# An mLSTM and MoE kernel: the decays' exponents from a TensorE product in place of a DMA broadcast

## The chip, the cores and the metric

The kernel runs on one core of a Trainium2 chip. The core has five engines with instruction queues of their own: PE (matrix products, results to PSUM), DVE, ACT and POOL (elementwise work and reductions) and SP, which here issues all DMA transfers; 16 DMA engines carry them. The metric is the time of one execution in microseconds of the device. Before the change it is 322.91 us, the median of three runs (322.81 to 323.3).

## The reference

Two stages follow each other. The first is a recurrent cell over 768 steps for 4 batches x 8 heads, head size 40, with gates that decay the state; the second is a feed-forward layer over the 3072 tokens with 320 features, 1024 hidden units, an activation h x softmax(h) and a layer norm.

```python
for t in range(S):
    m_new = np.maximum(f_gate[:, :, t] + m, i_gate[:, :, t])
    f_stab = np.exp(f_gate[:, :, t] + m - m_new)
    i_stab = np.exp(i_gate[:, :, t] - m_new)
    m = m_new
    C = f_stab[..., None, None] * C + i_stab[..., None, None] * np.einsum('bhd,bhe->bhde', vt, kt)
    n = f_stab[..., None] * n + i_stab[..., None] * kt
    h_tilde = np.einsum('bhde,bhe->bhd', C, qt)
    denom = np.maximum(np.abs(np.einsum('bhd,bhd->bh', n, qt)[:, :, None]), 1.0)
    y[:, :, t] = sigmoid(o_gate[:, :, t]) * h_tilde / denom
x = y.transpose(0, 2, 1, 3).reshape(B * S, H * D)
h = x @ w_in
e = np.exp(h - max(h)); solu = h * e / (sum(e) + 1e-09)
out = (solu - mean(solu)) / sqrt(var(solu) + 1e-06) * g_ln @ w_out
```

## The kernel before

The recurrence is worked in chunks of 128 steps, so there are 24 units: 4 batches x 6 chunks, chunk by chunk over the batches. With G the running sum of the forget exponents inside a chunk and I the input gate relative to the running maximum, step t sees step s of its chunk with the weight exp(G[t] + I[s] - G[s]) for t >= s, and 0 else.

**Head of the program.** The gates lie as 32 rows (batch and head) of 768 steps. Two scans on DVE (lines 393 and 409) give the maximum and G. G is stored to DRAM (tile gd, line 419). POOL subtracts to get I - G, PE transposes I - G and G, DVE copies both to bG (line 458), and ACT takes the exponential of the G half (line 461). Beside it the weights arrive as 64-bit words: ACT, DVE and PE decode, split, centre and scale them (load_w_in, load_w_out, centre_w_out, scale_w_out). Idle products on PE (line 1340) keep its clock up until the output weights' means are formed.

**One unit.** SP loads the tokens tk (v, k, q; line 803) and **gb** (line 804): G of the unit's chunk, 8 heads x 128 steps, read from DRAM into all 128 partitions. DVE finds the largest value of a token, am (line 829), ACT and DVE split k and q into two half-precision parts qs, and SP transposes them to qT by DMA (line 873). POOL writes -1e30 into gb where t < s (line 889). ACT makes the weights d: one exponential per head with I - G as the bias of each partition (line 904), and before the mask dec, the decay of the whole chunk, from gb's last column (line 885). PE forms the scores from qT into a PSUM tile sy (946), DVE multiplies them by am and d into p (958), PE multiplies p by the values into sy (1008) and qT by the state cs (982). DVE divides, giving x, and POOL multiplies by the sigmoid of the output gates sg (line 1058). For the next chunk POOL scales k by d's last column (kt, 926), PE multiplies it by the values (1072), POOL decays the state (ct, 1082), DVE adds (1094), POOL splits the state into parts (1107, 1116), and SP copies them across partitions (1122, 1123). Then the layer: PE transposes x (1132), 16 matmuls of 128x512 give ph (1185), DVE takes the negated row maximum nm (1201), ACT and DVE form e and its statistics, POOL takes a power (pw, 1262) and splits e into us (1277), SP transposes us by DMA into big (1282), and 24 matmuls give the output (1305).

**Order.** A planner (class Plan) simulates the engines with a cost for each operation and issues, on each engine, the ready operation of the lowest rank. Ranks come from the table RANK, one row per engine and tile, as base, slope at the head and slope at the tail. Nothing is reordered at run time. PSUM tiles are shared: sy has two buffers, sx and so_ one each, ph two.

Of the kernel before, what the change touches and what calls it, by code (L numbers as in the profile page):

```python
# [8 lines left out]
F32 = mybir.dt.float32  # L9
# [5 lines left out]
ALU = mybir.AluOpType  # L15
# [318 lines left out]
def mlstm_moe_kernel(ctx: ExitStack, tc: tile.TileContext, tok, og, fg, ig, w_in, w_out, gln, out):  # L334
# [81 lines left out]
    for b in range(B):  # L416
        load(
            300,
            lambda P, b=b: nc.sync.dma_start(
                out=P[("gd", 0)][b].rearrange("c h l -> h c l"),  # L420
                in_=gt(P, G_)[b * H : (b + 1) * H, :].rearrange("h (c l) -> h c l", l=L),
            ),
            [("gd", 0, b)],
            [G_],
            prio=g0,
        )

# [10 lines left out]
        POOL,  # L438
        1790,
        lambda P: nc.gpsimd.tensor_tensor(out=gt(P, I_), in0=gt(P, I_), in1=gt(P, G_), op=ALU.subtract),  # L440
        [I_],
        [G_],
        prio=g0,
    )
    for nm in SMALL:
        P.tag(nm, SMALL[nm], lambda nm=nm: pp.tile([L, 512], F32, name=nm, tag=nm, bufs=SMALL[nm]))

    def tr_gates(P):
        pt = P[("so_", "g")].rearrange("p (a c n) -> p a c n", a=2, c=8)
        for c in range(NC):  # L450
            nc.tensor.transpose(pt[:, 0, c, :], gt(P, I_)[:, c * L : (c + 1) * L], P[I][: B * H, : B * H])
            nc.tensor.transpose(pt[:, 1, c, :], gt(P, G_)[:, c * L : (c + 1) * L], P[I][: B * H, : B * H])

    P.op(PE, 700, tr_gates, [("so_", "g")], [I_, G_, I], prio=g0)


    def mk_bG(P):
        V.tensor_copy(out=P[BG], in_=P[("so_", "g")].rearrange("p (a c n) -> p a c n", a=2, c=8)[:, :, 0:NC, :])
# [14 lines left out]
    cst("wg", [L, NK, DM], F32)  # L473
# [3 lines left out]
    WIH, WIL, WOH, WOL, WG, OW = (("wih", 0), ("wil", 0), ("woh", 0), ("wol", 0), ("wg", 0), ("ow", 0))  # L477

# [23 lines left out]
    def decode(raw, n, key, dst, prio):  # L502
# [14 lines left out]
        def di(P):  # L517
# [21 lines left out]
            [key],  # L539
# [32 lines left out]
    def load_w_in(i, prio):  # L572
# [18 lines left out]
        load(1500, ld, [raw], prio=RANK["sp w_in"][0], behind=[("gb", 0)] if i > 2 else [])  # L591
# [156 lines left out]
    tag("gb", [L, H, L], F32, 2)  # L748
# [37 lines left out]
    def unit(u):  # L786
        b, c = units[u]
        pr = float(u)
        tk, gb, am, rr, qT, d_t = (("tk", u), ("gb", u), ("am", u), ("rr", u), ("qT", u), ("d", u))
# [13 lines left out]
        load(1500, lambda P: nc.sync.dma_start(out=P[tk], in_=tok[b, c * L : (c + 1) * L, :]), [tk], prio=rank(SPQ, "tk"), behind=[("gb", u - 2)] if u > 1 else [])  # L803
        load(1500, lambda P: nc.sync.dma_start(out=P[gb], in_=P[("gd", 0)][b, c].partition_broadcast(L)), [gb], [("gd", 0, b)], prio=rank(SPQ, "gb"))
# [78 lines left out]
        dec = ("dec", u)  # L883
        if 0 < c < NC - 1:
            op(ACT, 110, lambda P: nc.scalar.activation(out=P[dec], in_=P[gb][0:D, :, L - 1], func=AF.Exp), [dec], [gb])  # L885
        op(
# [3 lines left out]
                out=P[gb],  # L890
                in_=P[gb],
# [10 lines left out]
        def decay(P, j):
            for h in range(4 * j, 4 * j + 4):
                nc.scalar.activation(  # L904
                    out=P[d_t][:, h, :],
                    in_=P[gb][:, h, :],
                    func=AF.Exp,
                    bias=P[BG][:, 0, c, b * H + h : b * H + h + 1],
                )
# [11 lines left out]
        kt = ("kt", u)  # L921
# [464 lines left out]
```

## Time and profile before

| | |
|---|---|
| median of 3 runs | 322.91 us (322.81 to 323.3) |
| the profiled execution | 324.31 us, of which the span from first to last instruction is 322.5 us |
| granted PE clock, mean | 0.979 |
| busy share of the span | PE 87%, DVE 82%, ACT 74%, POOL 54% |
| DMA engines, share of their time | 89% |
| moved over the span | 66.66 MB |

A share is an average over a program with different stages. What a unit costs is read from stretches of the span, and from what an engine waited for just before it went on. PE's busy time includes the run-out of each matmul, so that its rate is read from the starts of successive ones.

### The profile page before, as it was taken

Reading aid. Unit: us, or ns where it says so; the run is one execution under the profiler, and the core shown is the slowest. Engines: PE = TensorE matmul, PEld = TensorE weight load, DVE = VectorE, ACT = ScalarE, POOL = GpSimd, SP = SyncE. Lnnn points to the kernel's source line nnn. Section 1 sums busy time; section 2 is a strip of 40 time slices with the busy share of each in tenths; the row PEclk is TensorE's granted clock in tenths of the full one; section 3 lists DMA queues with packets and bytes.
Section 4 is the critical chain, followed back from the end, with each engine's and each line's share of the span. In section 5 each row is a group of like instructions: output and inputs, shape, how many; then the busy total and the mean of one; then the engine's idle time right before and its main releaser. Section 6 shows DMA issues by size and latency. Waiting matters only on the chain.

```text
span 322.5 us, 6918 instructions
## 1 busy us (share of the span) xinstructions
PE 279.7 (87%) x2403; PEld 229.8 (71%) x2403; DVE 264.3 (82%) x671; ACT 239.7 (74%) x505; POOL 174.5 (54%) x186
## 2 busy tenths in 40 slices
PE   0189979697989999897999969999889989999984
PEld 0189868475868888686778848878767767888753
DVE  7978998999999888859969866988889889887740
ACT  2466788989788999649979847987869967635641
POOL 6435152638467847763848655666657655434210
PEclk9999988969999999999999997999999999999999
DMA  7599995899889999999989999999998999634391
GB/s 218 202 250 252 331 255 195 196 259 224 165 255 213 238 187 231 216 250 239 217 200 227 258 208 239 185 233 225 239 200 229 212 241 190 133 66 91 82 155 58
DMA packets 118723, 66.66 MB, mean 207 GB/s; under 512 B 102880, under 2 KB 110016, under 8 KB 118688
## 3 DMA queue, kind: packets, MB, share of 16 engines
q1 hardware_dynamic: 118688, 66.21, 89.0%
q8 instruction: 19, 0.31, 0.4%
q14 instruction: 16, 0.13, 0.2%
HBM read 33.85 MB, written 4.03 MB: 117 GB/s over the span
## 4 chain that ended last, share of the span: by engine, by line
PE 42%; DVE 14%; DMA 14%; issue 13%; POOL 9%; SPq 3%; ACT 3%; POOLq 0%; ACTq 0%; DVEq 0%
PE ph L1185 14%; DMA tk<-in_tok_dram 5%; PE sy L1008 4%; DMA gb<-gd 4%; PE sx L1132 2%; DMA big<-us 2%; POOL x L1058 2%; POOL gb L889 2%; PE sy L946 2%; PE sy L982 2%; PE sx L1072 1%; POOL us L1277 1%; DVE qs L857 1%; DMA out_dram<-ot 1%; DVE wg L547 1%
## 5 line engine op out<-in xcount | busy, mean ns | idle before, releaser
L1305 PEld LDWEIGHTS <-big 128*128 128x128 f16 x576 | 63.2, 118 | 18.0 <-DMA big<-us 3.8
L904 ACT ACTIVATE d<-gb,bG 128x128 f32<-128x128 f32 x192 | 59.0, 390 | 3.5 <-POOL gb L889 1.7
L1008 PEld LDWEIGHTS sy<-tk,p 128*128 128x128 f32 x384 | 57.4, 198 | 2.9 <-DVE p L958 0.3
L849 ACT ACTIVATE qs<-tk,rr 128x640 f16<-128x640 f32 x48 | 37.2, 819 | 26.7 <-DVE rr L842 23.2
L1008 PE MATMUL sy<-tk,p 128*128 128x41 f32 x384 | 56.6, 253 | 0.1
L1277 POOL TENSOR_TENSOR us<-e,us 128x1024 f16<-128x1024 f32 x23 | 49.1, 2139 | 11.0 <-ACT us L1287 10.8
L889 POOL TENSOR_SCALAR_AFFINE_SELECT gb<-gb 128x1024 f32<-128x1024 f32 x24 | 27.3, 1137 | 37.8 <-ACT dec L885 21.7
L829 DVE TENSOR_REDUCE am<-tk 128x1 f32<-128x640 f32 x24 | 19.5, 812 | 21.9 <-DMA tk<-in_tok_dram 21.9
L958 DVE SCALAR_TENSOR_TENSOR p<-sy,am,d 128x512 f32<-128x512 f32 x48 | 35.0, 736 | 2.4 <-PE sy L946 2.3
L1262 POOL TENSOR_TENSOR pw<-ab,mhalf 128x1 f32<-128x1 f32 x24 | 13.2, 551 | 42.4 <-DVE ab L1254 41.9
L1201 DVE TENSOR_REDUCE nm<-ph 128x1 f32<-128x1024 f32 x24 | 29.2, 1217 | 7.1 <-PE ph L1185 6.9
L1185 PE MATMUL ph<-wih,xh 128*128 128x512 f32 x96 | 34.1, 437 | 0.0
L1058 POOL TENSOR_TENSOR x<-x,sg 128x320 f32<-128x320 f32 x24 | 21.8, 908 | 20.3 <-DVE rr L842 7.8
L1243 ACT ACTIVATE sq<-e,nmean 128x1024 bf16<-128x1024 f32 x24 | 27.5, 1146 | 5.8 <-DVE e L1234 5.4
L1234 DVE SCALAR_TENSOR_TENSOR e<-ph,s,e 128x1024 f32<-128x1024 f32 x24 | 30.6, 1273 | 0.9 <-ACT e L1208 0.9
L1208 ACT ACTIVATE e<-ph,nm 128x1024 f32<-128x1024 f32 x24 | 26.6, 1109 | 5.0 <-DVE nm L1201 4.7
L1185 PE MATMUL ph<-wil,xh 128*128 128x512 f32 x96 | 30.1, 394 | 0.0
L857 DVE SCALAR_TENSOR_TENSOR qs<-tk,rr,qs 128x320 f16<-128x320 f32 x48 | 29.0, 633 | 0.5 <-ACT qs L849 0.3
L1287 ACT CAST us<-e 128x1024 f16<-128x1024 f32 x24 | 24.9, 1035 | 2.7 <-issue 2.6
L1185 PE MATMUL ph<-wih,xl 128*128 128x512 f32 x96 | 26.5, 398 | 0.2 <-DVE xl L1143 0.2
L926 POOL TENSOR_TENSOR kt<-tk,d 128x320 f32<-128x320 f32 x20 | 16.5, 829 | 11.9 <-ACT d L904 10.7
L1132 PE MATMUL sx<-ident,x 128*128 128x128 f32 (+1 forms) x72 | 12.8, 289 | 10.7 <-POOL x L1058 5.9
(181 smaller groups left out, 691.7 us busy)
## 6 DMA issues: line engine op xcount, KB each, us to landing
gb<-gd SPq DMA_DIRECT2D x24, 512.0 KB
tk<-in_tok_dram SPq DMA_DIRECT2D x24, 484.0 KB
sg<-in_og_dram SPq DMA_DIRECT2D x12, 320.0 KB
out_dram<-ot SPq DMA_DIRECT2D x24, 160.0 KB
big<-in_w_out_dram SPq DMA_DIRECT2D x4, 640.0 KB
cs<-cs SPq DMA_DIRECT2D x20, 102.5 KB
big<-in_w_in_dram SPq DMA_DIRECT2D x4, 512.0 KB
cs<-c SPq DMA_DIRECT2D x20, 51.2 KB
```

Of the source, the lines that this page charges most:

```text
L849: nc.scalar.activation(out=dst, in_=q_src(P, a).unsqueeze(2).to_broadcast([L, H, 2, D]), func=AF.Copy, scale=P[rr],)
L857: V.scalar_tensor_tensor(out=q_parts(P, a, 2 - a, 1), in0=q_src(P, a), scalar=P[rr], in1=q_parts(P, a, 0, 1), op0=ALU.mult, op1=ALU.subtract,)
L889: lambda P: nc.gpsimd.affine_select(out=P[gb], in_=P[gb], pattern=[[0, H], [1, L]], base=0, channel_multiplier=-1, compare_op=ALU.is_ge, f ...
L904: nc.scalar.activation(out=P[d_t][:, h, :], in_=P[gb][:, h, :], func=AF.Exp, bias=P[BG][:, 0, c, b * H + h : b * H + h + 1],)
L958: lambda P, j=j, ps=ps: V.scalar_tensor_tensor(out=P[p_t][:, 4 * j : 4 * j + 4, :], in0=P[ps].rearrange("p (h l) -> p h l", l=L), scalar=P ...
L1008: nc.tensor.matmul(yv(P)[:, h, :], lhsT=P[p_t][:, h, :], rhs=v1(P)[:, h, :], start=True, stop=True)
L1058: lambda P: nc.gpsimd.tensor_tensor(out=P[x], in0=P[x], in1=P[sg][:, u % OG, :], op=ALU.mult),
L1185: nc.tensor.matmul(P[ph][:, j * 512 : (j + 1) * 512], lhsT=a, rhs=w[:, j * 512 : (j + 1) * 512], start=n == 0, stop=n == 7,)
L1201: lambda P: V.tensor_reduce(out=P[nm], in_=P[ph], axis=AX.X, op=ALU.max, negate=True),
L1234: lambda P: V.scalar_tensor_tensor(out=P[e], in0=P[ph], scalar=P[sc], in1=P[e], op0=ALU.mult, op1=ALU.mult, accum_out=P[nmean]),
L1277: (V if last else nc.gpsimd).tensor_tensor(out=P[us[1]][:, 1], in0=P[e], in1=P[us[0]][:, 0], op=ALU.subtract)
L1305: nc.tensor.matmul(P[po][:, 0:DM], lhsT=uTv(P, a)[:, k, :], rhs=P[w][:, k, :], start=n == 0, stop=n == 23)
```

## The change

The exponent G[t] + I[s] - G[s] becomes a matrix product. Each of the two terms is split into a part rounded to the PE's 32-bit format and the rest. A left operand **el** of 128 rows x 128 steps holds two rows of ones, then two rows for each of the 8 heads with the parts of I - G, and zeros below. A right operand **er** of 128 rows x 8 heads x 128 steps holds in its first two rows the parts of G, below them indicators (one in the rows of the head, zero elsewhere), and zeros in the rest. Two matmuls of 128x512 per unit, four heads each, give the exponents in sy. Rows that never change are written once; per unit SP loads only el's 16 rows and er's 2 rows, 8 KB each, from two DRAM tiles bd and gd.

ACT takes the exponential from PSUM, two instructions of four heads each, with no bias. POOL's mask now works on d, after the exponential, and writes zeros. DVE writes p in place into d, so that the tile p is gone and d has three buffers. The last column of d is copied to dl on ACT before the mask, for kt. The decay of the state no longer comes from gb: a product with a selecting matrix (sel) copies exp(G) of each chunk's last step for all units to 40 partitions at once, in the head (tile DEC). In the head, I - G moves from POOL to DVE, and each of I - G and G gets a copy on ACT and a subtraction on DVE for its parts, and two stores. The state's own arithmetic is unchanged. The gates' scratch rows move into wg, which the output weights fill later.

The core of the diff (of RANK two rows; all others have new numbers too):

```diff
-    "sp gb": (-18.49, -14.13, -3.91),
+    "sp el": (-8.75, 8.76, 2.09),
...
+    def parts(whole, hi, dst):
+        P.op(ACT, 750, lambda P: nc.scalar.copy(out=gt(P, hi).bitcast(F32R), in_=gt(P, whole)), [hi], [whole], prio=g0)
+        P.op(DVE, 870, lambda P: V.tensor_tensor(out=gt(P, whole).bitcast(F32R), in0=gt(P, whole), in1=gt(P, hi), op=ALU.subtract), ...)
+        for n, k in enumerate((hi, whole)):
+            load(100, lambda P, n=n, k=k: nc.sync.dma_start(out=P[dst][:, n], in_=gt(P, k)), [(*dst, n)], [k], prio=g0)
...
+    parts(I_, BT, BD)
+    parts(G_, GH, GD)
...
-        load(1500, lambda P: nc.sync.dma_start(out=P[gb], in_=P[("gd", 0)][b, c].partition_broadcast(L)), ...)
+        load(100, lambda P: nc.sync.dma_start(
+                out=P[el].bitcast(F32)[2 : 2 + 2 * H],
+                in_=P[BD].rearrange("p a s -> (p a) s")[b * 2 * H : (b + 1) * 2 * H, c * L : (c + 1) * L]), ...)
+        load(100, lambda P: nc.sync.dma_start(
+                out=P[er].bitcast(F32)[0:2],
+                in_=P[GD][b * H : (b + 1) * H, :, c * L : (c + 1) * L].rearrange("h a l -> a h l")), ...)
...
+        for j in range(2):
+            pd = ("sy", ("d", u, j))
+            def exponents(P, j=j, pd=pd):
+                nc.tensor.matmul(P[pd], lhsT=P[el], rhs=P[er].rearrange("p h l -> p (h l)")[:, j * 512 : (j + 1) * 512], start=True, stop=True)
+            P.op(PE, 232, exponents, [pd], [el, er], rank(PE, "d"))
+            op(ACT, 600, lambda P, j=j, pd=pd: nc.scalar.activation(
+                    out=P[d_t][:, 4 * j : 4 * j + 4, :], in_=P[pd].rearrange("p (h l) -> p h l", l=L), func=AF.Exp), ...)
+        if c < NC - 1:
+            op(ACT, 115, lambda P: nc.scalar.copy(out=P[dl], in_=P[d_t][:, :, L - 1]), [dl], [(*d_t, 0), (*d_t, 1)])
...
-        for j in range(2):
-            op(ACT, 1170, lambda P, j=j: decay(P, j), [(*d_t, j)], [gb, BG])
...
-        p_t = ("p", u)
+        p_t = d_t
...
-    tag("d", [L, H, L], F32, 2)
+    tag("d", [L, H, L], F32, 3)
```

**What moves in the order.** On PE, in the middle of the program: `so__` is a unit's output product, `ph` the hidden product of the next, `sy<-qT` the scores of the one after. Before:

```order
L1305 LDWEIGHTS big
L1305 MATMUL so__2506<-woh,big 128x320
L1185 MATMUL ph<-wih,xh 128x512 x2
L1185 MATMUL ph<-wil,xh 128x512 x2
L1185 MATMUL ph<-wih,xh 128x512 x2
L1185 MATMUL ph<-wil,xh 128x512 x2
L1185 MATMUL ph<-wih,xl 128x512 x4
L1185 MATMUL ph<-wih,x_2539 128x512 x2
L1185 MATMUL ph<-wil,x_2539 128x512 x2
L1072 MATMUL sx<-tk,kt 40x41 x8
```

The same place after:

```order
L1436 LDWEIGHTS big
L1436 MATMUL so__2404<-woh,big 128x320
L1005 MATMUL sy<-er_97,el_106 128x512
L1316 MATMUL ph<-wih,xh 128x512 x2
L1316 MATMUL ph<-wil,xh 128x512 x2
L1316 MATMUL ph<-wih,xl 128x512 x4
L1005 MATMUL sy<-er_97,el_106 128x512
L1076 LDWEIGHTS qT
L1076 MATMUL sy<-qT 128x128
```

The hidden product was in one piece; now the two exponent matmuls of the next unit stand ahead of it and in it, and the scores of that unit cut it too.

On POOL, one unit of the middle (the mask is AFFINE_SELECT; numbers tell the units apart). Before:

```order
L889 AFFINE_SELECT gb_2287<-gb_2287 128x1024
L1262 TENSOR_TENSOR pw_2457<-ab_2454,mhalf_94 128x1
L1277 TENSOR_TENSOR us_2447<-e_2330,us_2447 128x1024
L1058 TENSOR_TENSOR x_2467<-x_2467,sg_1746 128x320
L926 TENSOR_TENSOR kt_2518<-tk_2194,d_2380 128x320
L1107 TENSOR_TENSOR cs0_2513<-cs0_2513 40x328
L1082 TENSOR_TENSOR ct_2543<-cs1_1963,dec_2072 40x328
L1116 TENSOR_TENSOR c3_2583<-cs0_2513 40x328
```

After:

```order
L1393 TENSOR_TENSOR pw_2204<-ab_2197,mhalf_112 128x1
L1031 AFFINE_SELECT d_2169<-d_2169 128x1024
L1056 TENSOR_TENSOR kt_2237<-tk_1842,dl_2202 128x320
L1213 TENSOR_TENSOR ct_2246<-cs0_1694,dec_208 40x328
L1238 TENSOR_TENSOR cs3_2235<-cs3_2235 40x328
L1247 TENSOR_TENSOR c3_2286<-cs3_2235 40x328
L1408 TENSOR_TENSOR us_2336<-e_2291,us_2336 128x1024
L1189 TENSOR_TENSOR x_2362<-x_2362,sg_1938 128x320
```

The mask worked on the load of a later unit and now works on the weights that DVE multiplies next; it stands behind pw, and the split us goes behind the state's work.

On SP, one unit. Before:

```order
L1282 DMA_TRANSPOSE big<-us 128x16x128
L803 DMA tk<-in_tok_dram 128x968
L1122 DMA cs_2695<-cs_2695 40x656
L1123 DMA cs_2695<-c_2765 40x328
L804 DMA gb<-gd 128x1024
L873 DMA_TRANSPOSE qT<-qs_68 128x16x128
L1326 DMA out_dram<-ot 128x320
```

After:

```order
L1413 DMA_TRANSPOSE big<-us 128x16x128
L1253 DMA cs_2402<-cs_2402 40x656
L1254 DMA cs_2402<-c_2486 40x328
L990 DMA_TRANSPOSE qT<-qs_81 128x16x128
L901 DMA tk<-in_tok_dram 128x968
L904 DMA el_106<-bd 16x128
L1457 DMA out_dram<-ot 128x320
L914 DMA er_97<-gd 2x8x128
```

One broadcast becomes two small loads, and the token load has moved behind the transposition of qs.

More of the change, by code (lines that the diff above doesn't have):

```diff
@@ L415, in mlstm_moe_kernel @@
     )
[L416 to L426, printed above, removed]
     P.op(
@@ L437, in mlstm_moe_kernel @@
     P.op(
-        POOL,
-        1790,
-        lambda P: nc.gpsimd.tensor_tensor(out=gt(P, I_), in0=gt(P, I_), in1=gt(P, G_), op=ALU.subtract),
+        DVE,
+        870,
+        lambda P: V.tensor_tensor(out=gt(P, I_), in0=gt(P, I_), in1=gt(P, G_), op=ALU.subtract),
         [I_],
@@ L538, in decode @@
             ),
-            [key],
+            [key, *(gates if key[0] == "wg" else [])],
             [wa],
@@ L589, in ld @@
                     )
-        load(1500, ld, [raw], prio=RANK["sp w_in"][0], behind=[("gb", 0)] if i > 2 else [])
+        load(1500, ld, [raw], prio=RANK["sp w_in"][0], behind=[(*GD, 1)] if i > 2 else [])
         decode(raw, HF, wf, lambda P: P[wf][:, 0:HF], prio)
@@ L880, in unit @@
         )
[L883 to L886, printed above, removed]
+        for j in range(2):
+            pd = ("sy", ("d", u, j))
+            def exponents(P, j=j, pd=pd):
+                nc.tensor.matmul(
+                    P[pd],
+                    lhsT=P[el],
+                    rhs=P[er].rearrange("p h l -> p (h l)")[:, j * 512 : (j + 1) * 512],
+                    start=True,
+                    stop=True,
+                )
+            P.op(PE, 232, exponents, [pd], [el, er], rank(PE, "d"))
+            op(
+                ACT,
+                600,
+                lambda P, j=j, pd=pd: nc.scalar.activation(
+                    out=P[d_t][:, 4 * j : 4 * j + 4, :],
+                    in_=P[pd].rearrange("p (h l) -> p h l", l=L),
+                    func=AF.Exp,
+                ),
+                [(*d_t, j)],
+                [pd],
+            )
+        kt, dl = ("kt", u), ("dl", u)
+        if c < NC - 1:
+            op(ACT, 115, lambda P: nc.scalar.copy(out=P[dl], in_=P[d_t][:, :, L - 1]), [dl], [(*d_t, 0), (*d_t, 1)])
+        P.op(
             POOL,
@@ L895, in unit @@
                 compare_op=ALU.is_ge,
-                fill=NEG,
+                fill=0.0,
             ),
-            [gb],
-            [dec] if 0 < c < NC - 1 else [],
-        )
[L902 to L909, printed above, removed]
-        for j in range(2):
-            op(ACT, 1170, lambda P, j=j: decay(P, j), [(*d_t, j)], [gb, BG])
+            [(*d_t, 0), (*d_t, 1)],
+            [],
+            rank(POOL, "d"),
+        )
         if u % OG == 0:
@@ L932, in unit @@
                 [kt],
[L933 removed]
+                [tk, dl],
             )
```

269 lines of the change are left out of this document (189 added, 80 removed).

## The prediction

> **What bounds the kernel now.** I read the page's busy times, queues and DMA issues first.
>
> ```profile
> PE 279.7 (87%) x2403; PEld 229.8 (71%) x2403; DVE 264.3 (82%) x671; ACT 239.7 (74%) x505; POOL 174.5 (54%) x186
> ...
> q1 hardware_dynamic: 118688, 66.21, 89.0%
> ...
> gb<-gd SPq DMA_DIRECT2D x24, 512.0 KB
> ```
>
> PE and the transfers are both near 90%, and the broadcast that goes away is 24 x 512 KB, 12.6 of 66.21 MB. Next I cut the span at the row reductions nm (line 1201) of units 4 and 20. Columns: stretch, its length, busy time of PE, PEld, DVE, ACT and POOL, granted clock, DMA share, GB/s. The row with (x16) counts nm alone; the last row is a stretch of 20 us.
>
> ```profile
> 0.00:46.00 46.00, 27.74 (x226) 26.03 (x227) 39.39 (x63) 27.64 (x53) 20.15 (x27) 1.00 0.87 245
> 46.00:100.20 54.20, 47.48 (x331) 37.87 (x329) 52.04 (x134) 47.88 (x111) 29.35 (x30) 0.91 0.87 222
> 100.20:280.50 180.30, 167.74 (x1570) 137.63 (x1570) 149.09 (x413) 146.19 (x311) 113.15 (x121) 0.99 1.01 219
> 280.50:322.50 42.00, 36.73 (x282) 28.24 (x280) 23.81 (x63) 18.02 (x32) 11.85 (x10) 1.00 0.47 94
> ...
> 100.20:280.50 180.30, 19.45 (x16) 0.99 1.01 219
> ...
> 180.00:200.00 20.00, 16.95 (x153) 13.72 (x152) 14.01 (x41) 13.16 (x36) 9.89 (x13) 0.91 1.01 234
> ```
>
> So there are three stages. In the **head**, up to 100.2, DVE is busy 39.4 + 52.0 = 91.4 us and sets the pace. In the **middle**, sixteen units take 180.3 us, 11.27 each; the DMA share is 1.01 and PE idles 180.30 - 167.74 = 12.56 us. In the **tail** the transfers are at 0.47 and PE leads. How short a middle unit can be is seen where PE never waits, from one unit's hidden product to the next (timeline of PE):
>
> ```profile
> 106.46 0.74 PE L1185 MATMUL ph<-wih,xh 128*128 128x512 f32 x2
> ...
> 116.67 0.74 PE L1185 MATMUL ph<-wih,xh 128*128 128x512 f32 x2
> 117.25 0.63 PE L1185 MATMUL ph<-wil,xh 128*128 128x512 f32 x2
> 117.72 0.62 PE L1185 MATMUL ph<-wih,xh 128*128 128x512 f32 x2
> ```
>
> A clean unit is 116.67 - 106.46 = 10.21 us of PE, so the middle loses 1.06 us per unit. What PE and DVE waited for there (us in total, times, longest), and one late token load on the chain:
>
> ```profile
> DVE am L829 <- DMA tk<-in_tok_dram: 21.3, 12, 3.8
> ...
> PE sx L1132 <- POOL x L1058: 4.8, 6, 1.3
> PE sy L946 <- DVE x L1046: 3.3, 2, 1.8
> PE sx L1132 <- DVE sb L1217: 2.5, 2, 2.1
> ...
> 215.14 4.50 DMA tk<-in_tok_dram
> ```
>
> PE's own waits (4.8 + 3.3 + 2.5 of 12.56) are for x and what precedes it. DVE executes in order and stands 21.3 us at am until tokens have landed; whatever it owes PE stands behind that. I read the middle as held by the transfers, with PE 1.06 us per unit behind them.
>
> **The change, part by part.** The groups that give the durations:
>
> ```profile
> L904 ACT ACTIVATE d<-gb,bG 128x128 f32<-128x128 f32 x192 | 59.0, 390 | 3.5 <-POOL gb L889 1.7 <-DVE s L1229 0.8 <-DVE z L1251 0.7
> L958 DVE SCALAR_TENSOR_TENSOR p<-sy,am,d 128x512 f32<-128x512 f32 x48 | 35.0, 736 | 2.4 <-PE sy L946 2.3
> L889 POOL TENSOR_SCALAR_AFFINE_SELECT gb<-gb 128x1024 f32<-128x1024 f32 x24 | 27.3, 1137 | 37.8 <-ACT dec L885 21.7 <-DMA gb<-gd 9.8 <-DMA cs<-cs 3.5
> ...
> L885 ACT ACTIVATE dec<-gb 40x8 f32<-40x8 f32 x16 | 3.2, 202 | 0.4 <-DMA gb<-gd 0.4
> ...
> L597 ACT CAST wih<-e 128x512 fp32r<-128x512 f32 x4 | 2.5, 614 | 3.4 <-DVE e L558 3.4
> ...
> L402 DVE TENSOR_TENSOR d<-p 32x767 f32<-32x767 f32 x1 | 0.9, 944 | 0.0
> ...
> L458 DVE COPY bG<-so__138 128x384 f32<-128x384 f32 x1 | 0.6, 551 | 0.0
> ```
>
> *Transfers.* No row times one broadcast on the 16 engines. By bytes at the middle's 219 GB/s it is 524 KB / 219 = 2.4 us; by its 128 packets of some 4945 per unit, 2.6% of 11.4 us, 0.3. I take 1.8, nearer the bytes, since its packets are the long ones. The middle's demand, 1.01 x 11.27 = 11.4 us per unit, falls to about 9.7 with the two 8 KB loads el and er that replace it (16 KB, 0.1 us by bytes).
>
> *PE.* Two matmuls of 128x512 per unit. Two in a row take 117.72 - 117.25 = 0.47 us. The first pair of a group takes 117.25 - 116.67 = 0.58, so a switch of operands can cost 0.11; the new order cuts the hidden product of each unit in one or two more places. I add 0.10 (0 to 0.25). In the head these matmuls fall into PE's waits and cost nothing.
>
> *ACT.* Eight activations, 59.0 / 24 = 2.46 us per unit, become two of 128x512 from PSUM. The cast of that size takes 0.61, so 1.2 us; at the small ones' rate it would stay 2.46, which I take as the other end and as far off, since one instruction has one start. The copy dl takes dec's place, 0.2 for 0.2. ACT sinks from 146.19 / 16 = 9.1 to 7.9 us per unit. ACT doesn't lead the middle, so this is cover, not gain.
>
> *POOL and DVE per unit.* The mask keeps its shape and price, 1.14 us, and so does p, 0.74 per half. But the mask moves behind the exponentials: PE exponents, ACT, POOL mask, DVE p now follow one another, with sy's two buffers shared by six uses per unit where there were four. Before, the mask needed only the load. The price of that is not in the trace: 0 where the new order leaves room, up to one mask, 1.1 us per unit, where it leaves none. I take nothing apart from the waits left below, and make the rest a rival.
>
> *SP's queue.* One more load per unit, about 0.44 us. This is a unit of SP in the middle, and two transposes issued when transfers were few:
>
> ```profile
> 205.19 3.18 SPq L1282 DMA_TRANSPOSE big<-us  x1
> 208.46 0.53 SPq L803 DMA_DIRECT2D tk<-in_tok_dram  x1
> 209.08 0.77 SPq L1122 DMA_DIRECT2D cs<-cs  x1
> 209.96 0.72 SPq L1123 DMA_DIRECT2D cs<-c  x1
> 210.78 3.17 SPq L873 DMA_TRANSPOSE qT<-qs  x1
> 214.04 0.54 SPq L804 DMA_DIRECT2D gb<-gd  x1
> 214.68 0.37 SPq L1326 DMA_DIRECT2D out_dram<-ot  x1
> 215.14 0.38 SPq L803 DMA_DIRECT2D tk<-in_tok_dram  x1
> ...
> 268.99 1.79 SPq L873 DMA_TRANSPOSE qT<-qs  x1
> ...
> 272.07 1.80 SPq L1282 DMA_TRANSPOSE big<-us  x1
> ```
>
> The queue is nearly solid, but 6.35 us of it are two transposes that need 3.59 when the engines are not full. I expect them in between, so the extra load is covered, and the tokens of 215.14, issued 1.1 us after a broadcast, land about the broadcast's 1.8 us sooner.
>
> *The waits left.* PE idled 12.56 / 16 = 0.79 us per unit. With demand 9.7 under a period near 11 most of it goes; I keep 0.27, a third (0 to 0.79).
>
> *The head.* DVE gains three tensor_tensors over the gates (one comes from POOL) at 0.94, and a copy of 40x192 takes the place of bG's 0.55 (between 0 and that, I take 0.35): +2.8 - 0.2 = 2.6 us on the engine that leads. Against this stand up to 100.2 - 91.4 = 8.8 us of DVE waits, 2 of them before the first gates arrive. Two waits for broadcasts are on the chain there, and the store that the new loads also need:
>
> ```profile
> 11.75 1.50 DMA gd<-us
> ...
> 18.59 5.68 DMA gb<-gd
> ...
> 33.15 5.71 DMA gb<-gd
> ```
>
> The new path needs two small landings (store, load; 1.5 each) before the first exponents, while DVE has weights to decode. I take back half of the 2.6: +1.3 (-2 to +4).
>
> *Sum.* Middle: 10.21 + 0.47 + 0.10 + 0.27 = 11.05 per unit against 11.27, times 16: -3.5. Tail: unit 23's two matmuls, +0.5. Head: +1.3. Together -1.7 us. The profiled execution itself took 324.31 us for a span of 322.5, 1.4 above the median 322.91; I apply the difference to the median: **321.2 us**. By the ends: all waits gone, no switches, head -2: 16 x (10.68 - 11.27) + 0.5 - 2 = -10.9; all waits kept, switches 0.25, head +4: 16 x (11.72 - 11.27) + 0.5 + 4 = +11.7.
>
> *A rule beside the clock.* Row first: between 180 and 200 the granted clock was 0.91, 1.8 us of full speed lost, where PE waited longest. The Trainium skill (TensorE: Matmul & The Clock Gate, What's actually happening) has the array drop to half speed after an idle window of about 3.4 us; one such window loses 1.7 us, and the trace agrees. By the rule that loss recurs unless waits thin out everywhere, and the sum would be 0.0, no change, in place of -1.7.
>
> **The rivals.** A gain or loss within 0.2%, 0.65 us, can't be told from none.
>
> - *More goes.* The transfers' relief clears all waits of the middle and the head's broadcasts with them: 16 x (10.78 - 11.27) + 0.5 - 1 = -8.3, 314.6 us. For it: PE's waits all trace to late tokens. Against: DVE's 91.4 busy us in the head only grow.
> - *SP takes over.* If transposes still issue in 3.2 us each, SP's unit grows by 0.44 to 11.7, tokens stay late, and PE's 0.57 hides in the wait: 16 x 0.44 + 1.3 + 0.5 = +8.8, 331.7 us. For it: the solid queue above, and that in the new order the token load stands behind the transposition of qs, 1.8 to 3.2 us further back. Against: the 1.8 us issues.
> - *The mask comes late (slower).* POOL is in order and in the new order the mask follows pw, which waits for the previous unit's statistics. If p then waits 0.5 us per unit with sy held, PE stops: +8 on my sum, 329.2 us. It decides from 1.7 / 16 = 0.11 us per unit. Against: POOL is at 113.15 of 180.3.
> - *Small loads cost like large ones.* If each of el and er held the engines for a landing of 1.5 us, demand would be 11.4 - 1.8 + 3.0 = 12.6 and the time +21, 344 us. Against: the trace keeps many small transfers in flight at a share of 1.01. The Trainium skill (DMA: Bandwidth & Descriptors, Rules for kernel authors) has this rule: below 64 KB a transfer is mostly overhead. No run here shows yet whether that overhead occupies the engines.
>
> **How the numbers follow.** Forecast 0.48 (its own range 317 to 326: faster 0.33, same 0.11, slower 0.04); more goes 0.19; SP 0.14; mask 0.15; small loads 0.02; something else slow 0.02. Faster is 0.33 + 0.19 = 0.52, same 0.11 plus a mild mask 0.01, slower the rest, 0.36. The range 313.5 to 331 leaves out the outer half of the SP case, the last two, and the outer parts of the gain and the mask, about 0.2 together.
>
> **What the profile after would show.** Right: middle units near 11.0 us, DMA share there below 0.92, DVE's wait for tokens under 7 us, exponent matmuls 0.23 us apart from their neighbours, exponentials near 0.6 us, transposes issued in under 3 us. Wrong: sy matmuls waiting on p, or p on POOL's mask, for over 0.3 us per unit (mask); SP solid and tokens late (SP); nm of unit 4 past 104 or before 98 (head).

## The result and the profile after

The changed kernel takes 315.09 us (median of four runs, 314.57 to 315.79) against 323.11 of the kernel before on the same chip (322.81 to 325.43): a ratio of 0.974 with an interval of 0.969 to 0.979, 8.0 us faster. The forecast was 1.7 us faster. The profiled execution took 315.54 us for a span of 313.8. Its page, busy times and the DMA queue:

```profile
PE 278.2 (89%) x2389; PEld 224.7 (72%) x2389; DVE 272.1 (87%) x674; ACT 214.2 (68%) x369; POOL 177.3 (56%) x194
...
q1 hardware_dynamic: 116400, 54.32, 78.3%
```

Cut again at nm of units 4 and 20 (stretch, length, busy PE, PEld, DVE, ACT, POOL, granted clock, DMA share, GB/s):

```profile
0.00:98.27 98.27, 69.60 (x527) 55.62 (x528) 91.36 (x195) 68.09 (x118) 48.50 (x58) 0.98 0.72 181
98.27:271.14 172.87, 171.51 (x1583) 140.83 (x1582) 156.32 (x418) 127.15 (x217) 116.62 (x126) 1.00 0.91 191
271.14:313.80 42.66, 37.10 (x283) 28.20 (x281) 24.43 (x63) 18.96 (x34) 12.12 (x11) 0.99 0.44 92
```

The middle went from 180.3 to 172.9 us, the head from 100.2 to 98.3, the tail from 42.0 to 42.7. In the middle a unit takes 10.80 us, and PE idles 172.87 - 171.51 = 1.36 us where it idled 12.56. All that PE waited for there, and DVE's longest waits (us in total, times, longest):

```profile
PE sx L1263 <- DVE so L1397: 0.9, 1, 0.9
PE sy L1005 <- ACT d L1017: 0.2, 1, 0.2
PE sy L1113 <- DVE d L1088: 0.2, 1, 0.2
...
DVE nm L1332 <- PE ph L1316: 7.1, 12, 1.0
DVE ab L1385 <- ACT sq L1374: 3.3, 9, 0.5
DVE am L946 <- DMA tk<-in_tok_dram: 1.1, 2, 0.8
DVE d L1088 <- POOL d L1031: 0.4, 2, 0.3
```

DVE's wait for tokens fell from 21.3 to 1.1 us, and DVE's longest wait is now for PE's hidden product. PE sets the middle. The new operations by groups (busy us, mean ns of one, then the idle time before them; a matmul's 472 ns contains its run-out):

```profile
L1088 DVE SCALAR_TENSOR_TENSOR d<-sy,am,d 128x512 f32<-128x512 f32 x48 | 33.6, 741 | 1.7 <-POOL d L1031 1.4 <-PE sy L1076 0.2
L1017 ACT ACTIVATE d<-sy 128x512 f32<-128x512 f32 x48 | 28.2, 590 | 11.3 <-PE sy L1005 11.0
L1031 POOL TENSOR_SCALAR_AFFINE_SELECT d<-d 128x1024 f32<-128x1024 f32 x24 | 27.0, 1125 | 23.0 <-DVE qs L974 16.1 <-ACT dl L1027 5.8 <-ACT d L1017 0.6
L1005 PE MATMUL sy<-er,el 128*128 128x512 f32 x48 | 22.5, 472 | 0.2 <-ACT d L1017 0.2
```

### The profile page after: what moved, and what is told of

It is laid out like the page before. It is cut to its first block, busy times and chain, and to the rows that moved or that the text cites. A ratio compares the mean times of both kernels' runs of the same rounds, so it can differ in the third digit from the quotient of the medians.

```text
span 313.8 us, 6764 instructions
## 1 busy us (share of the span) xinstructions
PE 278.2 (89%) x2389; PEld 224.7 (72%) x2389; DVE 272.1 (87%) x674; ACT 214.2 (68%) x369; POOL 177.3 (56%) x194
## 4 chain that ended last, share of the span: by engine, by line
PE 54%; DVE 26%; DMA 6%; POOL 4%; issue 4%; SPq 3%; ACT 2%; POOLq 0%; ACTq 0%; DVEq 0%
PE ph L1316 19%; PE sy L1139 6%; DMA tk<-in_tok_dram 3%; PE sx L1203 3%; DVE d L1088 2%; PE sy L1076 2%; PE sy L1005 2%; DVE qs L974 2%; PE sy L1113 2%; DVE am L946 2%; PE sx L1263 2%; DVE nm L1332 2%; DMA big<-us 2%; DVE e L1365 1%; POOL us L1408 1%
## 5 line engine op out<-in xcount | busy, mean ns | idle before, releaser
L1436 PEld LDWEIGHTS <-big 128*128 128x128 f16 x576 | 62.4, 117 | 15.9 <-issue 3.0
L1139 PEld LDWEIGHTS sy<-tk,d 128*128 128x128 f32 x384 | 55.5, 191 | 3.1 <-DVE d L1088 0.4
L1139 PE MATMUL sy<-tk,d 128*128 128x41 f32 x384 | 55.0, 248 | 0.0
L966 ACT ACTIVATE qs<-tk,rr 128x640 f16<-128x640 f32 x48 | 37.3, 821 | 15.2 <-DVE rr L959 14.9
L1031 POOL TENSOR_SCALAR_AFFINE_SELECT d<-d 128x1024 f32<-128x1024 f32 x24 | 27.0, 1125 | 23.0 <-DVE qs L974 16.1
L1017 ACT ACTIVATE d<-sy 128x512 f32<-128x512 f32 x48 | 28.2, 590 | 11.3 <-PE sy L1005 11.0
L1088 DVE SCALAR_TENSOR_TENSOR d<-sy,am,d 128x512 f32<-128x512 f32 x48 | 33.6, 741 | 1.7 <-POOL d L1031 1.4
L1339 ACT ACTIVATE e<-ph,nm 128x1024 f32<-128x1024 f32 x24 | 26.7, 1113 | 11.5 <-DVE nm L1332 11.4
L1316 PE MATMUL ph<-wih,xh 128*128 128x512 f32 x96 | 31.7, 411 | 2.5 <-ACT xh L1269 2.5
L1005 PE MATMUL sy<-er,el 128*128 128x512 f32 x48 | 22.5, 472 | 0.2 <-ACT d L1017 0.2
L1316 PEld LDWEIGHTS ph<-wih,xh 128*128 128x128 f32 x96 | 17.0, 189 | 6.5 <-ACT xh L1269 3.3
L1076 PE MATMUL sy<-qT 120*128 120x128 f16 x192 | 18.6, 224 | 2.7 <-DVE x L1177 1.9
```

Of the source, the lines that this page charges most:

```text
L966: nc.scalar.activation(out=dst, in_=q_src(P, a).unsqueeze(2).to_broadcast([L, H, 2, D]), func=AF.Copy, scale=P[rr],)
L1005: nc.tensor.matmul(P[pd], lhsT=P[el], rhs=P[er].rearrange("p h l -> p (h l)")[:, j * 512 : (j + 1) * 512], start=True, stop=True,)
L1017: lambda P, j=j, pd=pd: nc.scalar.activation(out=P[d_t][:, 4 * j : 4 * j + 4, :], in_=P[pd].rearrange("p (h l) -> p h l", l=L), func=AF.Exp,),
L1088: lambda P, j=j, ps=ps: V.scalar_tensor_tensor(out=P[p_t][:, 4 * j : 4 * j + 4, :], in0=P[ps].rearrange("p (h l) -> p h l", l=L), scalar=P ...
L1139: nc.tensor.matmul(yv(P)[:, h, :], lhsT=P[p_t][:, h, :], rhs=v1(P)[:, h, :], start=True, stop=True)
L1316: nc.tensor.matmul(P[ph][:, j * 512 : (j + 1) * 512], lhsT=a, rhs=w[:, j * 512 : (j + 1) * 512], start=n == 0, stop=n == 7,)
```

## The experiments

The theory: in the middle the broadcast's traffic made tokens late; without it the waits vanish and PE bounds, dearer by the exponent product. Rivals: the relief of ACT, the order found anew, the mask. For the head, where I had forecast a loss, the question was what gave 2 us. "Head" below ends at unit 4's nm and "unit" is a sixteenth of the time from there to unit 20's, both of the profiled execution, which can lie up to 2.9 us above the median of its run. The ratio is to the kernel before on the same chip. The rows come from several chips, on which the median of the kernel before was 322.2 to 323.6 us; a difference of about 1 us between two rows may be no more than that.

| run | median us | ratio and interval | head | unit | tail |
|---|---|---|---|---|---|
| before | 323.11 | 1 | 100.3 | 11.27 | 41.9 |
| after | 315.09 | 0.974 (0.969 to 0.979) | 98.3 | 10.80 | 42.7 |
| b_small_gb | 309.51 | 0.959 (0.952 to 0.966) | 100.7 | 10.32 | 42.0 |
| a_bcast_all | 345.85 | 1.071 (1.065 to 1.078) | 107.1 | 12.09 | 44.1 |
| a_bcast_cs | 336.99 | 1.044 (1.036 to 1.052) | 99.2 | 12.09 | 42.4 |
| a_small_all | 316.92 | 0.982 (0.977 to 0.987) | 99.4 | 10.80 | 42.6 |
| a_pe2 | 323.31 | 1.001 (0.998 to 1.004) | 99.5 | 11.21 | 43.0 |
| a_exp8 | 318.15 | 0.987 (0.981 to 0.993) | 99.4 | 10.86 | 45.4 |
| a_mask2 | 337.10 | 1.044 (1.034 to 1.054) | 105.9 | 11.60 | 44.8 |
| a_head_dve2 | 318.05 | 0.985 (0.979 to 0.992) | 101.1 | 10.78 | 42.7 |
| a_pool_busy | 320.18 | 0.993 (0.990 to 0.996) | 103.8 | 10.86 | 42.7 |
| a_old_rank | 368.21 | 1.139 (1.133 to 1.144) | 121.9 | 11.69 | 57.6 |
| a_old_rank_cs | 375.01 | 1.160 (1.152 to 1.168) | 123.2 | 12.21 | 57.5 |
| a_fold_mask | 315.42 | 0.975 (0.970 to 0.980) | 98.3 | 10.86 | 42.8 |

**The traffic alone, in the kernel before (b_small_gb).**

```diff
-nc.sync.dma_start(out=P[gb], in_=P[("gd", 0)][b, c].partition_broadcast(L))
+n = L if u < 2 else 2
+nc.sync.dma_start(out=P[gb][0:n], in_=P[("gd", 0)][b, c].partition_broadcast(n))
```

(gb's two buffers are fixed tiles here, so that what an earlier unit left in them is read.)

> The kernel before, with its gb loads from the third unit on shrunk from 128 partitions to 2 (512 KB to 8 KB); order, ACT, POOL and PE as before. The decays of those units come from stale rows of gb, so this times the traffic only. Transfers (what the broadcast took from the 16 DMA engines is the whole gain of the middle, and PE bounds next): the DMA share of the middle falls from 1.01 to about 0.92, a middle unit goes from 11.27 to about 10.4 (10.21 of PE and some waits), and the time to 323 - 16 x 0.85 - 2 = about 307 us, below the changed kernel's 315, since the two exponent matmuls aren't there. ACT (its relief from eight exponentials to two is the gain): nothing here relieves ACT, so 323, within 1 us. Order (the newly found order is the gain): 323 as well, within 2 us.

The middle of this run, and the group of am, before (line 829) and in this run (line 830):

```profile
100.65:265.72 165.07, 163.72 (x1570) 136.99 (x1571) 146.06 (x413) 146.35 (x311) 112.05 (x121) 1.00 0.93 193
...
L829 DVE TENSOR_REDUCE am<-tk 128x1 f32<-128x640 f32 x24 | 19.5, 812 | 21.9 <-DMA tk<-in_tok_dram 21.9
...
L830 DVE TENSOR_REDUCE am<-tk 128x1 f32<-128x640 f32 x24 | 19.4, 808 | 6.9 <-DMA tk<-in_tok_dram 6.9
```

The wait for tokens falls from 21.9 to 6.9 us over the span and the middle by 15.3 us, in the old order and with ACT's old 146 us. PE idles 165.07 - 163.72 = 1.35 us, as in the changed kernel. So ACT and order are not needed for the gain in the middle. From here to the changed kernel the middle grows by 172.87 - 165.07 = 7.8 us, 0.49 per unit: the price of two exponent matmuls, which nothing hides. The head stays where it was (100.7 against 100.3), against my -2: the broadcasts of the later head units cost nothing there.

SP's transposes of qs in the middle, before, with the small gb, after, and in the two runs below that put the broadcast back, a_bcast_all and a_bcast_cs (ns: least, median, most):

```profile
L873 SPq DMA_TRANSPOSE qT<-qs x16: 1786/3236/4630, 100.3 to 269.0; - x16
...
L874 SPq DMA_TRANSPOSE qT<-qs x17: 1577/1889/3008, 100.6 to 262.6; - x17
...
L990 SPq DMA_TRANSPOSE qT<-qs x16: 1780/2007/4471, 101.3 to 258.4; - x16
...
L999 SPq DMA_TRANSPOSE qT<-qs x16: 1621/2307/5100, 112.2 to 289.6; - x16
...
L991 SPq DMA_TRANSPOSE qT<-qs x16: 1818/3485/6230, 102.4 to 279.9; - x16
```

By the median they are longer with the broadcasts (3.24, 2.31 and 3.49 us) than without (1.89 and 2.01). The DMA share does not order them: it is 0.93 both with the small gb and in a_bcast_cs. The small gb leaves SP's issues as many as they were and relieves its queue, so the solid queue was a consequence and not a bound of its own.

**The traffic put back in the changed kernel**, into a tile that nothing reads: behind each er load (a_bcast_all), with 2 partitions in its place (a_small_all), and behind the state's copies (a_bcast_cs; 20 of the 24 units have these copies).

```diff
 nc.sync.dma_start(out=P[er].bitcast(F32)[0:2], in_=...)        # a_bcast_all; a_small_all with 2 for L
+nc.sync.dma_start(out=junk, in_=P[GD][b * H + u % H].rearrange("a s -> (a s)")[0:1024].partition_broadcast(L))
...
 nc.sync.dma_start(out=P[cn][2 * D :, 0], in_=P[c3])            # a_bcast_cs
+nc.sync.dma_start(out=junk, in_=...)
```

> The changed kernel, with a 512 KB broadcast of gate rows from DRAM into a tile that nothing reads put behind each unit's er load; all else as in the changed kernel. Transfers: the demand per middle unit goes back from 9.8 to 9.8 + 1.6 = 11.4 us, DVE waits for tokens again (over 10 us in the middle against 1.1), units of 11.2 to 11.5, and the time is 322 to 327 us. ACT or order: the time stays at 315 to 316.5 us, since ACT's work and the order are untouched.

> The same as the run with the broadcast put back, but with 2 partitions (8 KB) in place of 128: one more issue on SP per unit and no traffic to speak of. Transfers: 315 to 316 us. SP's queue (the count of issues is what costs): its queue is nearly solid, one more issue of 0.4 to 0.5 us per unit would show in full, 315 + 16 x 0.45 = 322 us.

> The changed kernel with the 512 KB broadcast put back once more (20 units, the last four without), now issued behind the state's copies cs, where the kernel before had its gb, and not behind er, ahead of the transposition of us, where it cost 30 us. Place (the large cost there came from the transposition of us queued right behind it): the middle goes to about the demand of 11.4 us, 16 x 0.6 + 2 on 315, 323 to 328 us. Order (the new order, found for light traffic, stands full engines less well than the old, wherever the broadcast goes): 335 us or more, units near 12.

The middle of the three in that order, then what PE and DVE waited for most in the middle of the last:

```profile
107.10:300.47 193.37, 178.06 (x1583) 144.37 (x1582) 156.77 (x418) 126.71 (x217) 116.79 (x126) 0.98 0.99 212
...
99.43:272.28 172.85, 171.48 (x1583) 140.73 (x1582) 156.24 (x418) 127.09 (x217) 116.63 (x126) 1.00 0.89 192
...
99.23:292.65 193.42, 179.61 (x1583) 147.06 (x1582) 156.48 (x418) 127.41 (x217) 116.85 (x126) 0.96 0.93 211
...
PE sy L1114 <- DVE d L1089: 10.5, 5, 2.9
...
DVE am L947 <- DMA tk<-in_tok_dram: 17.9, 8, 3.4
```

One more small load per unit costs the middle nothing (172.85 against 172.87), so neither SP nor the engines are held by it. Its median is 1.8 us longer, and the two intervals of the ratio overlap; the 1.1 us between the profiled executions lie all in the head. The broadcast itself takes more than the whole gain: the units go to 12.09 in both places, and not to the 11.2 to 11.5 that I expected. Both middles hold 15 broadcasts, so the place makes no difference there. The heads (107.1 against 99.2) do not compare places alone, since a_bcast_all issues nine broadcasts in its head and a_bcast_cs five. 337 us with units of 12.09 is what the order reading of a_bcast_cs named, and not the place reading.

The sums show where my expectation of 11.2 to 11.5 failed, and what of the cost can be due to the order. With the broadcast at cs, the middle has 193.42 - 179.61 = 13.8 us of PE idle, 12.4 more than without, and PE's same instructions take 179.61 - 171.51 = 8.1 us longer at a clock of 0.96. In the old order the same broadcast brought 11.2 us of idle (12.56 - 1.35) and 4.0 us of longer PE (167.74 - 163.72, clock 0.99). So the idle time that the broadcast brings is nearly the same in both (15 broadcasts against 14); it comes on top of PE's work and is not hidden by it. I had taken the longer of demand and PE, when it is PE's work plus the waits. Of the 5.3 us that the new order loses more (20.6 against 15.3), 1.2 are idle time and 4.1 are PE's longer instructions; why the clock fell further there stays open, and with it whether the order plays a part. The Trainium skill (TensorE: Matmul & The Clock Gate, What's actually happening) has the clock halve after an idle window of about 3.4 us. The trace agrees in the size: in a_bcast_cs PE stood from 136.94 to 139.12, and from 141 to 144 the granted clock was 0.50. It does not show an unbroken idle stretch of that length, as the longest in this middle is 2.9 us; nor does the clock follow the length alone, as a stretch of 2.55 us at 211 left it at 1.00.

**PE as the bound (a_pe2).**

```diff
-nc.tensor.matmul(P[pd], lhsT=P[el], rhs=..., start=True, stop=True)
+for _ in range(2):
+    nc.tensor.matmul(P[pd], lhsT=P[el], rhs=..., start=True, stop=True)
```

> The changed kernel with each exponent matmul issued twice (the second overwrites the first with the same values): 0.23 us more of PE per half, 0.47 per unit, and nothing else. PE bounds the middle: units go from 10.80 to 11.27, 16 x 0.47 = 7.5 us and about 1 more in the other stages, 323 to 324.5 us. Transfers still bound it at a share of 0.91: PE's extra falls into waits, 315 to 317.

```profile
99.47:278.84 179.37, 178.87 (x1618) 146.88 (x1617) 156.21 (x419) 127.27 (x218) 116.88 (x126) 1.00 0.83 185
```

The middle grows by 6.5 us: 16 x 0.47 = 7.5, less 0.9 of the idle time (1.36 to 0.50). PE is the bound, and the whole gain is gone (ratio 1.001): at twice the price on PE the change would be worth nothing.

**ACT's eight small exponentials (a_exp8).**

```diff
-nc.scalar.activation(out=P[d_t][:, 4*j : 4*j+4, :], in_=P[pd].rearrange("p (h l) -> p h l", l=L), func=AF.Exp)
+for n in range(4):
+    nc.scalar.activation(out=P[d_t][:, 4*j + n, :], in_=P[pd][:, n*L : (n+1)*L], func=AF.Exp)
```

> The changed kernel with each of its two exponentials per unit cut into four of 128x128, one per head, as the kernel before has them; same operands, planned cost and order. ACT's busy time per middle unit goes from 7.9 to about 9.2 us. Transfers and PE: ACT has room, but the mask and p come about 0.6 us later per half; at most +1.5 us, 315 to 316.6. ACT (relief of ACT is the gain): most of the 8 us are lost, 320 to 323 us.

```profile
L1018 ACT ACTIVATE d<-sy 128x128 f32<-128x128 f32 x192 | 37.0, 285 | 7.9 <-PE sy L1005 7.8
...
304.00:318.70 14.70, 8.67 (x50) 5.31 (x48) 1.40 (x3) 1.58 (x3) 0.55 (x1) 0.88 0.35 75
```

Neither expectation held. The median grew by 3.1 us. The profiled execution was the longest of the four (320.43, 4.9 above the changed kernel's); of these 4.9 us, 1.1 lie in the head, 1.0 in the middle, as transfers and PE say, and 2.8 in the tail, where the clock of the last stretch was 0.88. The other three took 317.9 to 318.2 us at a mean clock of 0.995 to 1.000, against 0.989, so they do not have all of that tail; where their 3 us lie is not shown. And the run restores less of ACT's work than I meant: one small exponential takes 285 ns where it took 390, 37.0 us in all and not 59.0. What differs is the source (PSUM) and the bias of each partition, which is gone. The Trainium skill (ScalarE: Activation LUTs, What ACT_TABLE_LOAD costs) puts such a bias operand at about 93 ns, which agrees with the 105 between the two; that the source plays no part is not shown. So this run does not decide about ACT; against the ACT theory b_small_gb stands alone, with all of ACT's old work.

**The mask doubled (a_mask2), and nearly removed (a_fold_mask).**

```diff
-nc.gpsimd.affine_select(out=P[d_t], in_=P[d_t], ...)
+for _ in range(2): nc.gpsimd.affine_select(out=P[d_t], in_=P[d_t], ...)    # a_mask2
...
-out=P[d_t], in_=P[d_t], ..., base=0
+out=P[d_t][96:L, :, 110:], in_=P[d_t][96:L, :, 110:], ..., base=110 - 96   # a_fold_mask
+# constants: el[18+t, s] = -2**20 where s > t; er[18+t, h, t] = 1, for t < 110
```

> The changed kernel with POOL's mask issued twice on the same d: 1.14 us more of POOL per unit, and p released so much later. The mask has room (p is not what PE waits for): POOL goes from 7.3 to 8.4 us of a 10.8 us unit, and the time stays within 315 to 317.5. The mask is at its edge (the rival of the prediction, only not yet over it): most of 1.14 us per unit shows, 320 to 333 us, with sy matmuls waiting on p.

> A version meant to beat both. The product of el and er uses 18 of 128 rows; the other 110 now carry the mask: row 18 + t holds -2^20 in el for s > t, and one in er's column t of each head. That masks columns 0 to 109 for no PE time, and POOL's mask shrinks from 128x1024 to 32 partitions x 8 x 18 (from 1.14 to about 0.3 us); constants are written once, some 2.5 us of POOL ahead of the gates' subtraction; order as in the changed kernel. The mask's chain (PE, ACT, POOL, DVE) holds head and tail, as the doubled mask's +7 and +2 us there say: 0.85 us less per unit takes 3 to 6 us off, 309 to 312.5, with the middle at 10.7 to 10.8 still, since PE bounds it. Only a longer mask hurts, a shorter one gives nothing (DVE's 91 us of work hold the head): 313.5 to 316.

The groups of p (written into d) with the doubled mask, and of the mask when folded into the product:

```profile
L1088 DVE SCALAR_TENSOR_TENSOR d<-sy,am,d 128x512 f32<-128x512 f32 x48 | 33.8, 746 | 22.6 <-POOL d L1031 22.6
...
L1046 POOL TENSOR_SCALAR_AFFINE_SELECT d<-d 32x144 f32<-32x144 f32 x24 | 8.9, 369 | 22.7 <-DVE qs L989 13.6 <-issue 3.8 <-ACT dl L1042 3.0
```

The second mask adds 24 x 1.12 = 26.9 us of POOL, and 22.6 of it come out as DVE's wait before p (1.4 in the changed kernel), 22.0 us in the time. The rival of the late mask was at its edge: by estimate the new order leaves it some 0.2 us per unit (26.9 less the 21.2 by which the wait grew, over 24). Yet a mask of 0.37 us gives nothing, 315.42 against 315.09: in the middle PE bounds, and in the head POOL writes the constants while DVE scans the gates, where the scan that gives G (line 422) takes 4.68 us instead of 2.57. That puts nm of unit 0 at 48.2 instead of 47.2, and nm of unit 4 comes at 98.3 in both; what the shorter mask alone would save there is not separated. It was meant to beat the changed kernel too and only equals it.

**The head: DVE's new subtractions twice (a_head_dve2), and POOL kept busy (a_pool_busy).**

```diff
-V.tensor_tensor(out=gt(P, whole).bitcast(F32R), in0=gt(P, whole), in1=gt(P, hi), op=ALU.subtract)
+for o in (gt(P, RS), gt(P, whole).bitcast(F32R)):                        # a_head_dve2, also for I - G
+    V.tensor_tensor(out=o, in0=gt(P, whole), in1=gt(P, hi), op=ALU.subtract)
...
+nc.gpsimd.memset(junk, 0.0)                                              # a_pool_busy, behind the write of wol
+for _ in range(9): nc.gpsimd.affine_select(out=junk, in_=junk, ...)
```

> The changed kernel with the three new subtractions on the gates in the head issued twice (first into a scratch row that is dead): 3 x 0.94 = 2.8 us more of DVE before the first unit. They are on the path that leads the head (the prediction's step): the first row maximum of unit 4 moves from 98.3-99.4 to 101-102, and the time to 317.5 to 318.5. DVE has waits there that hide them: 315 to 316.

> The changed kernel with ten writes of a 128x1024 tile that nothing reads put on POOL at about 10 us, in its idle stretch of 16 us between the gates and the first mask; nothing waits for them. A shared resource of POOL and DVE (the head of the kernel before lost it to POOL's masks and products, and the changed kernel gained there because POOL stands idle while DVE decodes): DVE's decoding steps and gate subtractions between 10 and 20 us go from 0.67 and 0.94 to 1.2 to 1.9 us, the head is 3 to 6 us longer, 318 to 321. No such resource: DVE's steps keep 0.67 and 0.94, and the time is 315 to 316.

2.8 us of DVE move unit 4 by 2.8 us and the time by 3.0. So the subtractions lie on the path, as the prediction had it. Most of what paid for them shows in the groups of DVE's decoding (up to 62 us), before and after; the shapes are the same:

```profile
L547 DVE SCALAR_TENSOR_TENSOR e<-big,e 128x512 int32<-128x512 int32 x5 | 6.2, 1242 | 0.1
L558 DVE SCALAR_TENSOR_TENSOR e<-big,e 128x512 int32<-128x512 int32 x5 | 4.1, 817 | 0.0
...
L646 DVE SCALAR_TENSOR_TENSOR e<-big,e 128x512 int32<-128x512 int32 x5 | 3.4, 672 | 0.0
L657 DVE SCALAR_TENSOR_TENSOR e<-big,e 128x512 int32<-128x512 int32 x5 | 3.5, 702 | 0.0
```

Over the head the two decoding lines take 18.1 us before (10.34 + 7.79) and 13.4 after (6.61 + 6.75). It isn't the traffic, since with the small gb they take 19.3 (10.34 + 8.92), and it doesn't need the new ranks, since with the old ones (a_old_rank, below) they take 13.9 (6.70 + 7.17). POOL stands idle there after: its first mask waits 16.1 us for qs (the group above; 20.1 with the old ranks). With POOL kept busy, first the head of that run, then some of its rows (start, us):

```profile
0.00:103.77 103.77, 69.50 (x527) 55.28 (x528) 97.17 (x195) 68.17 (x118) 66.52 (x68) 1.00 0.69 170
...
11.54 16.53 POOL L601 TENSOR_SCALAR_AFFINE_SELECT junk<-junk 128x1024 f32<-128x1024 f32 x8
...
12.10 0.78 DVE L962 TENSOR_REDUCE am<-tk 128x1 f32<-128x640 f32 x1
...
13.58 1.78 DVE L441 TENSOR_TENSOR us<-us 32x768 f32<-32x768 f32 x1
15.29 0.14 DVE L975 RECIPROCAL rr<-am 128x1 f32<-128x1 f32 x1
15.37 1.51 DVE L673 SCALAR_TENSOR_TENSOR e<-big,e 128x512 int32<-128x512 int32 x1
16.80 1.25 DVE L646 TENSOR_SCALAR e<-uc 128x512 int32<-128x512 int32 x1
17.98 0.94 DVE L457 TENSOR_TENSOR us<-us,d 32x768 fp32r<-32x768 f32 x1
```

The subtraction goes from 0.94 to 1.78 us, decoding steps from 0.66 to 1.51 and from 0.41 to 1.25, in the rows shown each by 0.84 to 0.85 or not at all; the reduction am keeps its 0.78. Nothing waits for POOL's writes: they end at 29.2, and POOL then stands 2.55 us until ACT's dl lets the first mask start. DVE's busy time in the head grows by 5.8 us (91.36 to 97.17), the head by 5.5 and the median by 5.1. So POOL's work makes single DVE instructions longer. The Trainium skill (Trainium Architecture — The Big Picture, What this means for kernel authors) has the two contend for one shared port pair, under an exclusive lock. A delay of one size or none agrees with a lock, but no run here shows the port.

**The old order (a_old_rank, and with the broadcast a_old_rank_cs).**

```diff
-    "pool d": (-15.57, 5.78, -9.77), "dve p": (-0.39, 13.83, -5.88), ...
+    "pool d": (-15.57, 5.78, -9.77), "dve p": (13.14, -7.12, 9.09), ...     # ranks of before where a name has one
```

> The changed kernel in the order that the ranks of the kernel before give (for names that both have; the new operations keep their new ranks, which were not found for this mix). Order is the gain of the head: the first row maximum of unit 4 goes from 98-99 back to 101 or later, and the time to 317 to 322, with the middle at 10.8 to 11.0, since PE and not the order bounds it. Order is not: 315 to 316. If the middle is over 11.2 without any wait for tokens, the order is worth as much there as the traffic.

> The run before, with the 512 KB broadcast put back behind the state's copies cs, as in the run that gave 337 in the new order. The new order stands full engines less well than the old: the middle is at 11.2 to 11.6, as the kernel before with the same traffic (11.27), and the time some 8 us below 337, 325 to 330. The order isn't the reason (the exponent product itself, or its two loads, make full engines cost more): 335 to 340, units near 12.1 again.

Both went far outside what was expected. POOL in the first of them, one place of the middle:

```profile
208.32 0.87 POOL L1189 TENSOR_TENSOR x<-x,sg 128x320 f32<-128x320 f32 x1 [6.59 <-DVE x L1177]
209.15 2.14 POOL L1408 TENSOR_TENSOR us<-e,us 128x1024 f16<-128x1024 f32 x1
211.23 1.10 POOL L1031 TENSOR_SCALAR_AFFINE_SELECT d<-d 128x1024 f32<-128x1024 f32 x1
```

POOL stands 6.6 us at x, with the mask behind it. That p waits for the mask in turn is little of the loss, 2.9 us over the span. In all 53 us are lost: 23.6 in the head, 14.1 in the middle and 14.9 in the tail; which waits make up the rest is not shown. The old ranks were found for another set of operations, so this shows only that the changed kernel needs ranks of its own. That a new order is not the source of the gain in the middle rests on b_small_gb. The broadcast adds 0.52 us per unit to the old ranks' 11.69 and 1.29 to 10.80; since PE idles 9.4 us in the old ranks' middle without it (186.97 - 177.59 in the windows), and part of it hides there, this pair says nothing on which order stands full engines better.

## Why the prediction was right in direction and short in size

The forecast was 6.3 us short. By the profiled executions, which differ by 8.7 us and not 8.0, 3.9 of the error lie in the middle and 3.3 in the head.

- *The bound of the middle*: right. With the traffic gone the waits go, with it back they return. By share times unit, the broadcast's engine time was 1.01 x 11.27 - 0.93 x 10.32 = 1.78 us (taken: 1.8, nearer the bytes). By the same sum against a_small_all (0.89 x 10.80) it is 1.6 us in a_bcast_cs and 2.4 in a_bcast_all, so that the 1.8 is no fixed price.
- *The waits left*: the term that failed. I kept 0.27 us per unit, a third; 1.36 / 16 = 0.085 are left. That is 3.0 us of the middle's 3.9 us of error. The rival "more goes" (314.6 us) had it, down to the middle's 10.78. That its total comes so near is in part luck: the 1 us that it took off the head was to come from the broadcasts there, and with the small gb the head is no shorter.
- *PE's products*: 0.47 right. Of the 0.10 for the switches of operands most was too much: 10.21 + 0.47 + 0.085 leaves 0.04 of 10.80. That is the other 1.0 us.
- *The head*: wrong in sign, 2.0 us shorter and not 1.3 longer. The gates' 2.6 us are on the path (a_head_dve2), but DVE's busy time stayed at 91.4: decoding took 4.8 us less where POOL is idle, while the splits qs took 1.9 more (11.7 against 9.8) and a scan 0.9 more. What made the head shorter is then DVE's waits, 6.9 us where they were 8.8; before, 4.7 of them were for PE (p, rd and nm), of which none over 0.2 us is left, and those for tokens grew from 0.6 to 2.5. That POOL's work stretches DVE's is shown (a_pool_busy), and that the relief in decoding needs neither the lighter traffic nor the new ranks. How much of it is due to the mask's new place and how much to the subtraction that left POOL was not separated, and no run isolates what shortened the waits.
- *The tail*: +0.5 forecast, +0.7 to 0.8 measured (42.7 against 41.9 to 42.0 by the two cuts).
- *ACT*: 590 ns per exponential (forecast 0.6), cover and not gain, as said. *The named signs*: DMA share 0.91 (below 0.92), token wait 1.1 us (below 7), transposes of qs issued in 2.0 us by their median (below 3), though up to 4.5; the exponent matmuls stand 0.23 to 0.36 us ahead of the next matmul; nm of unit 4 comes at 98.3, just inside 98 to 104.
- *SP takes over*, *small loads cost like large ones*: neither came. The Trainium skill (DMA: Bandwidth & Descriptors, Rules for kernel authors) calls a transfer below 64 KB mostly overhead. One more 8 KB load per unit cost the middle nothing, at a DMA share of 0.89 against 0.91, so such overhead did not occupy the engines here.
- *The mask*: by the estimate from a_mask2 it stayed clear of p by 0.2 us per unit only. My argument against it, POOL's 113 of 180 busy us, was weak: a busy share says little on an in-order chain.
- *The clock*: 1.00 in the middle, so the loss at 180 to 200 did not recur. The sum in which it does recur, no change, fell because the waits thinned out, the condition that was set beside it. The loss came after PE stood 1.78 us at 189 and was short of work until 194; no unbroken idle stretch of 3.4 us stood ahead of it.

## What to carry to other kernels

Where transfers make tokens late, an in-order engine's waits add to the leading engine's work; relieve the transfers and nearly all of that goes at once, while what you pay on the leading engine is paid in full (here 15.3 us relieved, 7.8 paid). Price an operation's new place by what stands ahead of it on its in-order engine, and test the margin by doubling it. Where POOL works beside DVE, look at DVE's durations, not only at its waits.

## What was not expected of the hardware

- The DMA engines' busy share is no fixed demand: share times unit was 11.4, 11.2 and 12.0 us with the broadcasts in three places (before, a_bcast_cs, a_bcast_all), 9.6 to 9.8 without.
- POOL's work stretched single DVE instructions by 0.84 us, and POOL's own eight writes took 16.53 us, 2.07 each, beside DVE, where its masks take 1.1.
- A transpose by DMA holds SP longer beside the broadcasts: 3.24 us by its median before and 3.49 in a_bcast_cs, 1.89 with the small gb, the last two at the same DMA share of 0.93.
